# One attention-and-experts kernel on one core: scores moved ahead of the transposes, products of ones in the first groups, and smaller last batches

## The chip, the core and the metric

The kernel runs on one core of one Trainium2 chip. The metric is device time in microseconds. Three runs of the kernel before gave 682.09 us in the median (680.95 to 684.87). All data are float32 in memory.

## What is computed

A blockwise attention over 64-token chunks, then a mixture of eight experts in which each token goes to its best expert only. Cut to what matters:

```python
# attention: batch 8, heads 8, sequence 576, head width 64; chunks of 64 tokens
scores = scale * q_c @ k_c.T                 # 64 x 64 per chunk and head
attn   = exp(scores - max(scores))
attn   = attn / (sum(attn) + 1e-9)
x      = (attn @ v_c) -> [4608 tokens, 512]  # heads side by side

# experts: D = 512, F = 1024, E = 8
logits = x @ w_gate
e      = argmax(logits);  p = softmax(logits)[e]
y      = p * (relu(x @ w1[e]) @ w2[e])
```

## The kernel before, in words

**Tiles and groups.** The 4608 tokens are 36 tiles of 128 rows. Attention works on groups of two tiles, so there are 18 groups. The main loop (L899) runs one turn for each group g, and one turn touches three groups: the scores and softmax of g, the transposes and values of g-1 (called `ga`), and the routing input of g-2 (called `gl`). The order of the instructions on each engine is the order of this code: a manual schedule holds it for TensorE (PE), VectorE (DVE), ScalarE (ACT) and GpSimd (POOL). Each engine works through its own list in order and waits where an input or a buffer is not ready. Transfers of q, k, v and the first expert's weights go out on SP's list, three groups ahead.

**One turn before the change.** PE: transposes of the attention of g-1 (`attn_t`, L265, into the banks T and Q), the routing sums of g-3 (`sel_`, L864), the scores of g (`scores`, L222, into the pair of banks S), the transposes of x of g-2 (`x_t`, L297, again into T and Q), if a batch is due the matmuls of its token places (L369 to L374, into bank K), the products with v of g-1 (`attn_v`, L274, pair X), and the gate logits of g-2 (`logits`, L309). DVE: the row sums of g-1 (`su`, L249), the row maxima of g (`mx`, L235), the subtraction that writes `ex` (L238) and frees the scores' banks, the reciprocal `ri` (L257) and the scaling that writes x of g-1 (`x_out`, L286). ACT: copies out of T and Q (L266 `at`, L299 `xT`), a cast of half a weight chunk (`cast`, L81), the exponential of g (L244), and the copy `lp` of the gate logits (L873), which `sel_` reads one turn later.

**Routing.** When the last group of a batch has passed `sel_`, `route` (L314) is started as a generator. It works out the expert of each token, a place in an expert-sorted buffer `xd`, and the gate, in some 12 small DVE steps, and ends with one indirect DMA per tile on POOL (L406, here called a scatter) that writes the rows of x to `xd`. `BATCHES` gives the tiles of each batch. `advance("c")`, `advance("t")`, `advance("a")` and `pauses()` release steps of the generator that belong to PE or ACT or wait; `small_op(n)` releases up to n of the DVE steps.

**The end of attention.** The first slot of 256 rows (slot 0) is cut into 32 half steps; `filler(n)` lets PE do n of them between the steps of the last routing. After the last route `tables()` finds the rows and the experts of all later slots; POOL then gathers the rows of slot 1 (L508) and loads the weights of slot 2 (L493). From then on slots of 256 rows (some with 64 or 128 extra rows) follow one another to the end: two matrix products in three float32r passes each (L551, L558, L627 to L629), an output row scaled by its gate (L633) and scattered to the output (L634).

Of the kernel before, what the change touches and what calls it, by code (L numbers as in the profile page):

```python
# [8 lines left out]
F32 = mybir.dt.float32  # L9
# [9 lines left out]
P = 128  # L19
NT = 4608  # L20
# [5 lines left out]
NG = NTILE // G  # L26
RB = 4
XB = 5
BATCHES = [4, 8, 8, 4, 4, 4, 4]
NBAT = len(BATCHES)  # L30
NMAX = max(BATCHES)
EARLY = 3
# [13 lines left out]
def attn_moe_kernel(ctx: ExitStack, tc: tile.TileContext, q, k, v, wg, w, out):  # L46
# [86 lines left out]
    pw = bank("X", [P, P])  # L133
    for _ in range(WARM):
        nc.tensor.matmul(pw, ones, ones, start=True, stop=True)
    iota_i = xg[0][0][:, 0:BLK].bitcast(I32)
    nc.gpsimd.iota(iota_i, pattern=[[1, BLK]], base=0, channel_multiplier=0)
    pid_i = xg[0][1][:, 0:NTILE].bitcast(I32)
    nc.gpsimd.iota(pid_i, pattern=[[P, NTILE]], base=0, channel_multiplier=1)
    wg_sb = kv.tile([P, 4, 32], F32, name="wg_sb")  # L140
# [10 lines left out]
        nc.gpsimd.memset(rows_b[:, b:b + 1], float(BATCHES[b] * P))  # L151


    iota_f = const.tile([P, BLK], F32, name="iota_f")
    nc.vector.tensor_copy(iota_f, iota_i)
    pid = kv.tile([P, NTILE], F32, name="pid")
    nc.vector.tensor_copy(pid, pid_i)
# [52 lines left out]
    def quads(i, hp):  # L210
        for c in range(2):
            for m in range(2):
                o = hp * 128 + c * 64
                yield (slice(c * 64, (c + 1) * 64), m, slice((i * 4 + hp) * 64, (i * 4 + hp + 1) * 64),
                       slice(m * 64, (m + 1) * 64), slice(o, o + 64), (m * 64, c * 64))

    def scores(g):
        ps = pair["S"]
        for i in range(G):
            for hp in range(4):  # L220
                for po, m, fo, pi, fi, at_ in quads(i, hp):
                    nc.tensor.matmul(ps[po, m, fo], qt[g][pi, i, fi], kb[g % NK][pi, i, fi],  # L222
                                     start=True, stop=True, tile_position=at_)
        return ps
# [35 lines left out]
    def attn_t(ex):  # L260
        at = sp.tile([P, G, 4, 128], F32, name="at", bufs=1)
        for i in range(G):
            pt = bank("TQ", [P, 4, 128])
            for hp in range(4):
                nc.tensor.transpose(pt[:, hp, :], ex[:, i * 4 + hp, :, :].rearrange("p m k -> p (m k)"), ident)  # L265
            nc.scalar.copy(at[:, i, :, :], pt)  # L266
        return at
# [46 lines left out]
    def route(b, pl):  # L314


        t0, n = first[b], BATCHES[b]
        S3 = [P, n, E]

        xts = [(i, xb[(t0 + i) // RB % XB]) for i in range(0, n, RB)]  # L320
        vec = nc.vector

        def small(name, dt=F32, k=E):
            return sm.tile([P, NMAX, k], dt, name=name, bufs=2)[:, 0:n, :]

        def flat(x):
            return x.rearrange("p t o -> p (t o)")

        ft = sm.tile([P, NMAX, 2], F32, name="ft", bufs=2)[:, 0:n, :]
        nc.gpsimd.tensor_copy(ft[:, :, 1:2], pid[:, t0:t0 + n].unsqueeze(2))  # L330
        yield "c"
        lg = small("lg")
        nc.scalar.copy(lg, pl[:, 0:n, :])
        yield None
        yield "v"
        lm = small("lm", k=1)
        vec.tensor_reduce(flat(lm), lg, AX.X, ALU.max)
        yield "v"
        vec.tensor_tensor(lg, lg, lm.broadcast_to(S3), ALU.subtract)
        yield "v"  # L340
        io3 = iota_m8.unsqueeze(1).broadcast_to(S3)
        eq = small("eq")
        vec.scalar_tensor_tensor(eq, lg, 0.0, io3, ALU.is_equal, ALU.mult)
        yield "v"
        am = small("am", k=1)
        vec.tensor_reduce(flat(am), eq, AX.X, ALU.min)
        yield "v"
        o5 = oh_b[:, b, 0:n + 1, :]
        o4 = o5[:, 0:n, :]
        vec.tensor_tensor(o4, io3, am.broadcast_to(S3), ALU.is_equal)  # L350
        yield "v"
        lo = sm.tile([P, E, NMAX], BF16, name="lo", bufs=2)[:, :, 0:n]
        S8 = [P, E, n]
        vec.tensor_tensor(lo, am.rearrange("p t o -> p o t").broadcast_to(S8),
                          iota_m8.unsqueeze(2).broadcast_to(S8), ALU.is_lt)
        yield "v"
        pfx = sm.tile([P, E], BF16, name="pfx", bufs=2)
        with nc.allow_low_precision("whole numbers"):
            vec.tensor_reduce(pfx, lo, AX.X, ALU.add)
        yield "a"  # L360
        eg = small("eg")
        nc.scalar.activation(eg, lg, AF.Exp)
        yield "t"
        r_live[0] = True
        o = b % 2 * (NMAX + 1) * E
        pr = pR[:, o:o + n * E].rearrange("p (a b) -> p a b", b=E)
        pn = pR[:, o:o + (n + 1) * E].rearrange("p (a b) -> p a b", b=E)

        nc.tensor.matmul(pn, tri, o5, start=True, stop=False)  # L369
        for j in range(n):  # L370
            nc.tensor.matmul(pn[:, j + 1:n + 1, :], ones, o4[:, j:j + 1, :].broadcast_to([P, n - j, E]),
                             start=False, stop=False)
        nc.tensor.matmul(pr, ones, pfx.unsqueeze(1).broadcast_to([P, n, E]), start=False, stop=False)
        nc.tensor.matmul(pn, ones[0:1, :],  # L374
                         rowbase[0:1, b:b + 1].unsqueeze(2).broadcast_to([1, n + 1, E]),
                         start=False, stop=True)
        yield "a"
        nc.scalar.activation(cb[:, b, :], pn[:, n, :], AF.Copy, bias=-float(t0 * P))
        nc.scalar.activation(ce[:, :, b], pn[:, n, :], AF.Copy, bias=-float(t0 * P))
        if b == EARLY - 1:  # L380
            g = early()
            active.append([g, next(g), True])
        if b == NBAT - 1:
            g = tables()
            active.append([g, next(g), True])
        yield "v"
        gs = small("gs", k=1)
        vec.tensor_reduce(flat(gs), eg, AX.X, ALU.add)
        yield "v"
        vec.tensor_scalar(gs, gs, 1e-9, None, ALU.add)  # L390
        yield "v"
        vec.reciprocal(ft[:, :, 0:1], gs)
        yield "v"

        dst = small("dst")
        vec.tensor_tensor(dst, pr, o4, ALU.mult)
        r_live[0] = False
        yield "v"
        di = small("di", I32, 1)
        with nc.allow_low_precision("whole numbers"):  # L400
            vec.tensor_reduce(flat(di), dst, AX.X, ALU.add)
        stored.update(range(t0, t0 + n))
        for i, x in xts:
            nc.gpsimd.tensor_copy(x[:, :, D:D + 2], ft[:, i:i + RB, :])
        for i in range(n):
            nc.gpsimd.indirect_dma_start(  # L406
                out=xds[b % 2 * NMAX + i],
                out_offset=bass.IndirectOffsetOnAxis(ap=di[:, i, :], axis=0),
                in_=xts[i // RB][1][:, i % RB, :], in_offset=None, bounds_check=NT - 1, oob_is_err=False)

    active = []
    r_live = [False]
# [463 lines left out]
    def pauses():  # L876
        for x in list(active):
            if x[1] is None:
                x[1] = next(x[0], "end")
                if x[1] == "end":  # L880
                    active.remove(x)
# [6 lines left out]
    def cast(g):  # L888

        j = g - 2  # L890
        if 0 <= j < 16:
            split_half(j // 2, j % 2, j // 4 % 2)
        j = g + 1
        if 0 < j < 16:
            load_q(j)
# [3 lines left out]
    for g in range(NG):  # L899
        ga, gl = g - 1, g - 2  # L900
        pace[0] = 1000
        if ga >= 0:
            at = attn_t(st_e[ga])
        if gl >= 1:
            sel_(gl - 1)
            advance("c")
        ps = scores(g)
        if gl >= 0:
            st_x[gl] = x_t(gl, xb[gl * G // RB % XB])
        cast(g)  # L910
        if ga >= 0:
            su = soft_c(st_e.pop(ga))
        pauses()
        small_op(5)
        st_e[g] = soft_a(ps)
        soft_b(st_e[g])
        advance("t")
        advance("a")
        small_op(5)
        if ga >= 0:  # L920
            px = attn_v(ga, at)
        logits(gl)
        if ga >= 0:
            ri = soft_d(su)
            x_out(ga, px, ri, xb[ga * G // RB % XB])
        small_op(2)
        advance("a")
        side_op(4)
        if g + 3 < NG:
            load_qk(g + 3)  # L930
        if 3 <= g + 2 < NG:
            load_v(g + 2)

    g = NG - 1
    at = attn_t(st_e[g])
    sel_(g - 2)
    advance("c")
    st_x[g - 1] = x_t(g - 1, xb[(g - 1) * G // RB % XB])
    su = soft_c(st_e.pop(g))
    pauses()  # L940
    small_op(5)
    px = attn_v(g, at)
# [4 lines left out]
    advance("a")  # L947
    make_xt(0, banks="SS")
    sel_(g - 1)
    filler(1)  # L950
    advance("t")
    advance("a")
    st_x[g] = x_t(g, xb[g * G // RB % XB])
    small_op(5)
    filler(2)
    logits(g)
    filler(2)
    sel_(g)
    advance("c")
    pauses()  # L960
    small_op(7)
    advance("a")
    filler(3)
    advance("t")
    advance("a")
    small_op(5)
# [156 lines left out]
```

## Time and profile before

| what | value |
|---|---|
| median of 3 runs | 682.09 us |
| the profiled execution's own time | 682.78 us |
| its span, first to last instruction | 680.9 us |
| PE busy | 604.7 us, 89% of the span |
| DVE busy | 422.2 us, 62% |
| ACT busy | 285.6 us, 42% |
| POOL busy | 262.7 us, 39% |
| first `mx` of attention / last `mx` | 9.0 us / 157.3 us |
| scaling of the last group's x ends | 170.4 us |
| first matmul of slot 1 (L558) | 209.15 us |
| mean granted PE clock | 0.928 |

A timeline row gives the start, the length, the engine, the line, what is written from what, and in brackets how long the engine stood idle just before and what ended that. "issue" and "remote" name no engine of this program as the releaser. A window row gives for one stretch the busy time of each engine, the granted PE clock, the busy share of the DMA engines and their rate. In the records one float32 matmul of the program can show as two, so a `x64` there is the `x32` of the program.

### The profile page before, as it was taken

The numbers are of one execution on the slowest core, as the hardware profiler recorded it, in microseconds if no ns is written. First come the engines' busy times: TensorE is split into PE (matmuls) and PEld (weight loads), VectorE is DVE, ScalarE is ACT, GpSimd is POOL, SyncE is SP. The second block draws the span as 40 slices with busy tenths as digits, with TensorE's granted clock in tenths as the row PEclk, the third lists the DMA queues.
The fourth block names the chain that finished last, engine by engine and source line by source line (L and its number), as shares of the span: only waits on it lengthen the run. The fifth ranks groups of instructions, "written<-read, shape, count | busy, mean of one in ns | idle before, by whom it ended". The sixth has DMA issues, their size and how long they took to land. (4 is left out here: it accounts for less than half of the span.)

```text
span 680.9 us, 14512 instructions
## 1 busy us (share of the span) xinstructions
PE 604.7 (89%) x5757; PEld 529.4 (78%) x5757; DVE 422.2 (62%) x819; ACT 285.6 (42%) x523; POOL 262.7 (39%) x268
## 2 busy tenths in 40 slices
PE   5777878678897979999979999999999999999990
PEld 5566657466787868998859888998899898999980
DVE  5786738484454656776636646667555676667660
ACT  2554426253212334544425434445434444555540
POOL 2123332535261442653315415355313464256331
PEclk7898859697797989999999999999999999999996
DMA  8988857633155532224503612156631126221100
GB/s 311 354 297 275 277 204 252 227 98 116 65 172 210 184 121 96 76 65 161 168 6 128 201 65 59 31 176 204 225 97 34 55 84 230 83 66 34 33 3 31
DMA packets 31872, 94.91 MB, mean 139 GB/s; under 512 B 11456, under 2 KB 11456, under 8 KB 28160
## 3 DMA queue, kind: packets, MB, share of 16 engines
q0 software_dynamic: 20848, 60.74, 26.6%
q1 hardware_dynamic: 10896, 32.53, 13.9%
q8 instruction: 73, 1.20, 0.7%
q14 instruction: 55, 0.45, 0.2%
HBM read 122.65 MB, written 19.82 MB: 209 GB/s over the span
## 5 line engine op out<-in xcount | busy, mean ns | idle before, releaser
L75 DVE TENSOR_TENSOR wlo<-raw,whi 128x1024 fp32r<-128x1024 f32 x134 | 163.7, 1222 | 39.5 <-ACT whi L74 33.1
L493 POOL DMA_INDIRECT raw<-in_w,widx x71 | 72.9, 1026 | 214.4 <-DVE wlo L75 166.9
L74 ACT CAST whi<-raw 128x1024 fp32r<-128x1024 f32 x134 | 140.2, 1046 | 0.1
L571 ACT ACTIVATE hh<-psS 128x256 fp32r<-128x256 f32 x106 | 40.7, 384 | 169.3 <-PE psS L551 89.3
L551 PE MATMUL psS<-xhi,whi 128*128 128x256 f32 x328 | 93.6, 285 | 0.9 <-DVE xlo L534 0.7
L551 PE MATMUL psS<-xhi,wlo 128*128 128x256 f32 x328 | 93.3, 285 | 0.0
L551 PE MATMUL psS<-xlo,whi 128*128 128x256 f32 x328 | 93.3, 284 | 0.0
L576 DVE SCALAR_TENSOR_TENSOR hl<-psS,hh 128x256 fp32r<-128x256 f32 x106 | 44.7, 422 | 70.1 <-ACT hh L571 40.0
L508 POOL DMA_INDIRECT xg<-xd,idx x58 | 77.1, 1329 | 20.2 <-issue 15.8
L551 PEld LDWEIGHTS psS<-xhi,whi 128*128 128x128 f32 x328 | 63.3, 193 | 4.8 <-issue 1.1
L634 POOL DMA_INDIRECT out_y<-y,oid x40 | 49.5, 1237 | 44.1 <-DVE y L633 38.3
L551 PEld LDWEIGHTS psS<-xlo,whi 128*128 128x128 f32 x328 | 63.2, 193 | 2.5
L551 PEld LDWEIGHTS psS<-xhi,wlo 128*128 128x128 f32 x328 | 63.2, 193 | 0.0
L82 POOL TENSOR_TENSOR wlo<-raw,whi 128x512 fp32r<-128x512 f32 x16 | 20.3, 1271 | 92.8 <-ACT whi L81 64.1
L627 PE MATMUL psL<-whi,hh 128*128 128x512 f32 x136 | 55.5, 408 | 0.1
L627 PE MATMUL psR<-whi,hh 128*128 128x512 f32 x136 | 54.3, 399 | 0.0
L628 PE MATMUL psL<-wlo,hh 128*128 128x512 f32 x136 | 54.3, 399 | 0.0
L628 PE MATMUL psR<-wlo,hh 128*128 128x512 f32 x136 | 54.2, 398 | 0.0
L629 PE MATMUL psL<-whi,hl 128*128 128x512 f32 x136 | 53.7, 395 | 0.0
L629 PE MATMUL psR<-whi,hl 128*128 128x512 f32 x136 | 53.7, 395 | 0.0
L235 DVE TENSOR_REDUCE mx<-psS 128x16 f32<-128x1024 f32 x18 | 22.0, 1222 | 42.3 <-PE psS L222 20.2
L222 PE MATMUL psS<-kb,qt 64*64 64x64 f32 x1152 | 32.6, 253 | 10.6 <-issue 8.4
(224 smaller groups left out, 1234.2 us busy)
## 6 DMA issues: line engine op xcount, KB each, us to landing
vb<-in_v SPq DMA_DIRECT2D x18, 512.0 KB, 6.0
kb<-in_k SPq DMA_DIRECT2D x17, 512.0 KB, 5.3
qt<-in_q SPq DMA_DIRECT2D x17, 512.0 KB, 6.0
raw<-in_w SPq DMA_DIRECT2D x16, 256.0 KB, 5.4
raw<-in_w,widx POOLq DMA_INDIRECT x71
xg<-xd,idx POOLq DMA_INDIRECT x58
out_y<-y,oid POOLq DMA_INDIRECT x40
kb<-in_k SPq DMA_DIRECT2D x2, 256.0 KB, 4.4
```

The costliest lines, as they stand in the source:

```text
L74: nc.scalar.copy(hi, src)
L75: nc.vector.tensor_tensor(lo, src, hi.bitcast(F32), ALU.subtract)
L222: nc.tensor.matmul(ps[po, m, fo], qt[g][pi, i, fi], kb[g % NK][pi, i, fi], start=True, stop=True, tile_position=at_)
L493: nc.gpsimd.indirect_dma_start(out=raw[c][:, :], out_offset=None, in_=w, in_offset=bass.IndirectOffsetOnAxis(ap=widx[:, u, c:c + 1], axis= ...
L508: nc.gpsimd.indirect_dma_start(out=t[:, :], out_offset=None, in_=xd[0:rows, :], in_offset=bass.IndirectOffsetOnAxis(ap=place(u, h), axis=0 ...
L551: nc.tensor.matmul(ph, a, b[:, kc, 0:BLK], start=kc + i == 0, stop=kc + i == 5)
L571: nc.scalar.activation(hh, ph, AF.Relu)
L576: nc.vector.scalar_tensor_tensor(hl, ph, 0.0, hh.bitcast(F32), ALU.max, ALU.subtract)
L627: nc.tensor.matmul(py, hh, wh, start=f == 0, stop=False)
L628: nc.tensor.matmul(py, hh, wl, start=False, stop=False)
L629: nc.tensor.matmul(py, hl, wh, start=False, stop=f == 7)
L634: nc.gpsimd.indirect_dma_start(out=outs[m], out_offset=bass.IndirectOffsetOnAxis(ap=oid[u % 3][0:n, m:m + 1], axis=0), in_=y, in_offset=No ...
```

## The change

1. In each turn `scores(g)` stands first. `sel_` of g-3 follows, and only then `attn_t` of g-1, with the row sums of g-1 right behind it. The weight cast stands behind the exponential of g instead of ahead of it, and the first five small DVE steps of a turn, together with `pauses()`, stand behind the subtraction.
2. A new helper `keep(n)` issues n matmuls of ones with ones (128 x 512, bfloat16) into bank K. It runs behind the scores of group 0 with n = 12 and of group 1 with n = 6.
3. The last batch of four tiles becomes two batches of two, with the slices in `route` adapted. `iota_f` shrinks from 256 to 128 columns.
4. Behind the last group the fillers are shared out anew: one half step each between the steps of the last two batches, and the transposes of the last x (`x_t`) come ahead of the first filler.

```diff
-BATCHES = [4, 8, 8, 4, 4, 4, 4]
+BATCHES = [4, 8, 8, 4, 4, 4, 2, 2]
...
+    def keep(n):
+
+        for _ in range(n):
+            nc.tensor.matmul(pR.rearrange("p (a b) -> p a b", b=P), ones,
+                             ones.unsqueeze(1).broadcast_to([P, 4, P]), start=True, stop=True)
...
-        if ga >= 0:
-            at = attn_t(st_e[ga])
+        ps = scores(g)
+        keep((12, 6, 0)[min(g, 2)])
         if gl >= 1:
             sel_(gl - 1)
             advance("c")
-        ps = scores(g)
+        if ga >= 0:
+            at = attn_t(st_e[ga])
+            su = soft_c(st_e.pop(ga))
         if gl >= 0:
             st_x[gl] = x_t(gl, xb[gl * G // RB % XB])
-        cast(g)
-        if ga >= 0:
-            su = soft_c(st_e.pop(ga))
-        pauses()
-        small_op(5)
         st_e[g] = soft_a(ps)
         soft_b(st_e[g])
+        cast(g)
         advance("t")
         advance("a")
+        pauses()
         small_op(5)
...
     make_xt(0, banks="SS")
     sel_(g - 1)
+    advance("t")
+    advance("c")
+    st_x[g] = x_t(g, xb[g * G // RB % XB])
+    advance("a")
+    pauses()
+    small_op(5)
     filler(1)
+    logits(g)
+    small_op(7)
+    advance("a")
+    filler(1)
+    sel_(g)
+    advance("c")
     advance("t")
     advance("a")
-    st_x[g] = x_t(g, xb[g * G // RB % XB])
     small_op(5)
-    filler(2)
-    logits(g)
-    filler(2)
-    sel_(g)
-    advance("c")
     pauses()
+    filler(1)
     small_op(7)
     advance("a")
-    filler(3)
+    filler(1)
     advance("t")
     advance("a")
     small_op(5)
```

The order on PE over one whole turn in the middle of attention, before (psS holds the scores, `ex` the exponentials, xb and vb are x and v):

```order
L265 MATMUL psT<-ident,ex 128x128 x4
L265 MATMUL psQ<-ident,ex 128x128 x4
L864 MATMUL psL<-sel_g,lp 128x8 x2
L222 MATMUL psS<-kb_124,qt 64x64 x32
L297 MATMUL psT<-ident,xb_121 128x128 x4
L297 MATMUL psQ<-ident,xb_121 128x128 x4
L274 MATMUL psX<-vb_126,at 64x64 x32
L309 MATMUL psL<-xT_1056,wg_sb 32x256 x4
```

The same turn on PE in the changed kernel, whose lines stand some six further down:

```order
L228 MATMUL psS<-kb_124,qt 64x64 x32
L870 MATMUL psL<-sel_g,lp 128x8 x2
L271 MATMUL psT<-ident,ex 128x128 x4
L271 MATMUL psQ<-ident,ex 128x128 x4
L303 MATMUL psT<-ident,xb_121 128x128 x4
L303 MATMUL psQ<-ident,xb_121 128x128 x4
L280 MATMUL psX<-vb_126,at 64x64 x32
L315 MATMUL psL<-xT_1079,wg_sb 32x256 x4
```

The scores went from the middle of the turn to its head, the routing sums with them, and the two users of the banks T and Q (L271 and L303) now stand back to back.

ACT over the same turn, before (`at` and `xT` are the copies out of T and Q, `whi` the weight cast, `lp` what the routing sums read):

```order
L266 COPY at<-psT 128x512
L266 COPY at<-psQ 128x512
L299 COPY xT_1056<-psT 128x4x128
L299 COPY xT_1056<-psQ 128x4x128
L81 CAST whi_2_70<-raw_67 128x512
L251 ACTIVATE su<-su 128x16
L244 ACTIVATE ex<-ex 128x1024
L873 COPY lp<-psL 128x256
```

and in the changed kernel:

```order
L272 COPY at<-psT 128x512
L272 COPY at<-psQ 128x512
L257 ACTIVATE su<-su 128x16
L305 COPY xT_1079<-psT 128x4x128
L305 COPY xT_1079<-psQ 128x4x128
L250 ACTIVATE ex<-ex 128x1024
L81 CAST whi_2_70<-raw_67 128x512
L879 COPY lp<-psL 128x256
```

The weight cast moved from ahead of the exponential to between it and `lp`; so `lp`, which the routing sums ahead of the next transposes read, is now one instruction later behind the exponential.

PE behind the last group, before: the routing sums of the last group (L864) and what follows (psS<-xhi and psX<-whi are half steps of slot 0; the token places of the last batch come behind three more such rows):

```order
L864 MATMUL psL<-sel_g,lp 128x8 x2
L551 MATMUL psS<-xhi,whi_2_70 128x256
L551 MATMUL psS<-xlo,whi_2_70 128x256
L551 MATMUL psS<-xhi,wlo_2_78 128x256
L551 MATMUL psS<-xhi,whi_3_71 128x256
L551 MATMUL psS<-xlo,whi_3_71 128x256
L551 MATMUL psS<-xhi,wlo_3_79 128x256
L627 MATMUL psX<-whi_4_72,hh 128x512
L628 MATMUL psX<-wlo_4_80,hh 128x512
L629 MATMUL psX<-whi_4_72,hl 128x512
```

and in the changed kernel (L375 to L380 into psK are token places, here of the last batch but one):

```order
L870 MATMUL psL<-sel_g,lp 128x8 x2
L375 LDWEIGHTS tri
L375 MATMUL psK<-oh_b,tri 128x24
L377 LDWEIGHTS ones
L377 MATMUL psK<-oh_b,ones 128x16
L377 LDWEIGHTS ones
L377 MATMUL psK<-oh_b,ones 128x8
L379 LDWEIGHTS ones
L379 MATMUL psK<-pfx,ones 128x16
L380 LDWEIGHTS ones
L380 MATMUL psK<-rowbase,ones 128x24
```

Behind the last routing sums the places of a batch of two tiles now follow at once, and those of the very last batch after two more half steps. In all, the last batch's places have four half steps of slot 0 ahead of them on PE, where they had eight.

More of the change, by code (lines that the diff above doesn't have):

```diff
@@ L135, in attn_moe_kernel @@
         nc.tensor.matmul(pw, ones, ones, start=True, stop=True)
-    iota_i = xg[0][0][:, 0:BLK].bitcast(I32)
-    nc.gpsimd.iota(iota_i, pattern=[[1, BLK]], base=0, channel_multiplier=0)
+    iota_i = xg[0][0][:, 0:P].bitcast(I32)
+    nc.gpsimd.iota(iota_i, pattern=[[1, P]], base=0, channel_multiplier=0)
     pid_i = xg[0][1][:, 0:NTILE].bitcast(I32)
@@ L151, in attn_moe_kernel @@
         nc.gpsimd.memset(rows_b[:, b:b + 1], float(BATCHES[b] * P))
-    iota_f = const.tile([P, BLK], F32, name="iota_f")
+    iota_f = const.tile([P, P], F32, name="iota_f")
     nc.vector.tensor_copy(iota_f, iota_i)
@@ L318, in route @@
         S3 = [P, n, E]
-        xts = [(i, xb[(t0 + i) // RB % XB]) for i in range(0, n, RB)]
+        xts = [(i, min(RB, n), xb[(t0 + i) // RB % XB], (t0 + i) % RB) for i in range(0, n, RB)]
         vec = nc.vector
@@ L402, in route @@
         stored.update(range(t0, t0 + n))
-        for i, x in xts:
-            nc.gpsimd.tensor_copy(x[:, :, D:D + 2], ft[:, i:i + RB, :])
+        for i, m, x, r in xts:
+            nc.gpsimd.tensor_copy(x[:, r:r + m, D:D + 2], ft[:, i:i + m, :])
         for i in range(n):
@@ L408, in route @@
                 out_offset=bass.IndirectOffsetOnAxis(ap=di[:, i, :], axis=0),
-                in_=xts[i // RB][1][:, i % RB, :], in_offset=None, bounds_check=NT - 1, oob_is_err=False)
+                in_=xb[(t0 + i) // RB % XB][:, (t0 + i) % RB, :], in_offset=None, bounds_check=NT - 1, oob_is_err=False)
     active = []
@@ L934, in attn_moe_kernel @@
     g = NG - 1
-    at = attn_t(st_e[g])
     sel_(g - 2)
     advance("c")
+    at = attn_t(st_e[g])
+    su = soft_c(st_e.pop(g))
     st_x[g - 1] = x_t(g - 1, xb[(g - 1) * G // RB % XB])
-    su = soft_c(st_e.pop(g))
     pauses()
```

## The prediction

> **What bounds the kernel now.** I read the 40 slices first, then windows cut at the starts of the maxima `mx`, one per group.
>
> ```profile
> PE   5777878678897979999979999999999999999990
> PEclk7898859697797989999999999999999999999996
> ```
>
> From the 13th slice on (204 us) PE is busy nine tenths or more nearly throughout. From there to the end the slots pass on PE, and the change touches nothing in them; they move as a block. Whatever is to be won lies ahead of the first slot's matmuls at 209.15 us. There PE is at 5 to 8 tenths.
>
> ```profile
> 17.00:24.00 7.00, 4.50 (x105) 3.88 (x96) 4.79 (x7) 2.23 (x3) 0.00 (x0) 0.76 1.03 409
> 56.00:62.20 6.20, 4.93 (x150) 4.18 (x150) 5.01 (x6) 4.09 (x8) 1.27 (x1) 0.90 0.88 245
> 62.20:69.00 6.80, 5.79 (x162) 4.99 (x163) 6.07 (x12) 4.21 (x9) 1.41 (x2) 1.00 0.89 286
> 75.70:92.70 17.00, 11.95 (x193) 9.24 (x196) 5.97 (x12) 4.22 (x10) 9.37 (x11) 0.70 0.71 247
> 114.70:131.30 16.60, 11.41 (x186) 7.81 (x190) 7.75 (x20) 4.32 (x11) 9.62 (x12) 0.83 0.60 226
> ```
>
> The columns are the window, its length, then busy time of PE, PE's weight loads, DVE, ACT, POOL, the granted clock, the DMA share and GB/s. An undisturbed group takes 6.2 us, in which PE works 4.93 and DVE 5.01: neither is full, so a chain through both sets the pace. A group with routing steps takes 6.8 with DVE at 6.07. And two groups take 17: those in which eight tiles are scattered. The undisturbed group in order of time:
>
> ```profile
> 57.25 1.22 DVE L238 TENSOR_TENSOR ex<-psS,mx 128x1024 f32<-128x1024 f32 x1
> 58.51 1.06 ACT L244 ACTIVATE ex<-ex 128x1024 f32<-128x1024 f32 x1 [0.70 <-DVE ex L238]
> 59.47 0.35 ACT L873 COPY lp<-psL 128x256 f32<-128x256 f32 x1
> 59.62 0.66 PE L265 MATMUL psT<-ident,ex 128*128 128x128 f32 x4 [1.27 <-ACT ex L244]
> 60.37 0.58 ACT L266 COPY at<-psT 128x512 f32<-128x512 f32 x1 [0.54 <-PE psT L265]
> 60.55 0.51 PE L864 MATMUL psL<-sel_g,lp 128*128 128x8 f32 x4
> 60.99 1.16 PE L222 MATMUL psS<-kb,qt 64*64 64x64 f32 x64
> 62.08 0.66 PE L297 MATMUL psT<-ident,xb 128*128 128x128 f32 x4
> 62.22 1.22 DVE L235 TENSOR_REDUCE mx<-psS 128x16 f32<-128x1024 f32 x1 [1.07 <-PE psS L222]
> 63.10 1.16 PE L274 MATMUL psX<-vb,at 64*64 64x64 f32 x64
> 64.20 0.64 PE L309 MATMUL psL<-xT,wg_sb 128*32 128x256 f32 x8
> ```
>
> Subtraction, exponential, transposes, routing sums, scores, maxima, subtraction: 57.25 to 63.5, one group. PE waits 1.27 us for the exponential, DVE 1.07 for the scores. But these scores need nothing of that exponential; only their place behind its transposes makes them wait.
>
> **Term A, the start.**
>
> ```profile
> 8.25 0.69 PE L222 MATMUL psS<-kb,qt 64*64 64x64 f32 x32 [2.11 <-DMA qt<-in_q]
> 12.61 1.22 DVE L249 TENSOR_REDUCE su<-ex 128x16 f32<-128x1024 f32 x1 [1.12 <-ACT ex L244]
> 12.63 1.11 PE L265 MATMUL psT<-ident,ex 128*128 128x128 f32 x4 [3.69 <-ACT ex L244]
> 14.53 1.96 PE L222 MATMUL psS<-kb,qt 64*64 64x64 f32 x64
> 16.56 1.22 DVE L235 TENSOR_REDUCE mx<-psS 128x16 f32<-128x1024 f32 x1 [2.73 <-PE psS L222]
> 202.87 0.39 PE L628 MATMUL psX<-wlo,hh 128*128 128x512 f32 x1
> 203.10 0.39 PE L629 MATMUL psX<-whi,hl 128*128 128x512 f32 x1
> ```
>
> The 12 products start at 8.94 us. Matmuls 512 wide start 0.23 apart at full clock (202.87 and 203.10, far off but the nearest of that width), so 12 take 2.8, and about 5.2 at half. The scores of group 1 follow at 11.7 and take 1.16 (the 60.99 row) instead of 1.96. DVE has its row sums until 13.83, so the maxima start there instead of 16.56: **2.7 us**. At half clock they would start at 8.94 + 5.2 + 1.96 = 16.1: 0.5. The six later products delay the first transposes to about 14, and the cover is that DVE is in maxima and subtraction until 16.3; without that cover they cost 1.4. Bounds 0.5 to 2.7 less 1.4, so -0.9 to 2.7; I take 2.7, because the records show full clock at 8.25 (0.69 us for 32).
>
> The Trainium skill, "TensorE: Matmul & The Clock Gate", Part 1, knows a full and a half clock only, the half one after some 3.4 us idle. PE idles 3.69 us here and its transposes then take 1.11 instead of 0.66, so the trace agrees; by that rule the products hold the clock and the sum keeps its 2.7, and if products of ones did not count as work it would get the 0.5.
>
> **Term B, the ordinary groups.** Scores at the head of the turn take the loop above apart. Three loops are left. DVE: 5.0 of work plus routing steps. PE: pitch between starts 0.93 (transposes) + 0.44 + 1.09 + 1.02 + 1.10 + 0.65 = 5.2; to that comes a new wait, since `x_t` now follows the other transposes directly and needs the banks that `at` copies empty: first bank free at 0.75 + 0.58 = 1.33 behind the first transposes, PE there at 0.93: 0.4. So 5.6 to 5.8. And a chain over two groups: subtraction, exponential, then the new wait of the routing sums for `lp`, which now has the weight cast ahead of it (about 1.0 us behind the exponential), sums 0.44, transposes and copies 1.8, the x transposes, values 1.1, `x_out` 1.2, row sums 1.15, maxima 1.26, subtraction 1.22: 10.8 to 11.5, or 5.4 to 5.8 a group. Queued behind the waiting sums are both transposes and so `at`; the early scores give DVE work meanwhile. So 5.8 against 6.2, with routing steps 6.3 against 6.8; ten such intervals at 0.4 to 0.7: **5 us**. All idle time of DVE in them (say 1.1 each) would be 11; if the `lp` wait and the bank wait are not covered (1.0 + 0.4 against the 1.27 saved) it is -1. I take 5, near the rows of DVE.
>
> **Term C, the scatters.**
>
> ```profile
> 81.21 1.02 POOL L406 DMA_INDIRECT xd<-xb,di  x1 [0.86 <-DVE ri L257]
> 82.52 0.36 PE L222 MATMUL psS<-kb,qt 64*64 64x64 f32 x5 [0.39 <-issue]
> 90.21 0.97 POOL L406 DMA_INDIRECT xd<-xb,di  x1 [0.31 <-issue]
> 92.59 1.76 PE L274 MATMUL psX<-vb,at 64*64 64x64 f32 x51 [0.93 <-issue]
> 92.69 1.22 DVE L235 TENSOR_REDUCE mx<-psS 128x16 f32<-128x1024 f32 x1 [9.55 <-remote]
> 98.87 1.99 PE L222 MATMUL psS<-kb,qt 64*64 64x64 f32 x64
> 100.93 1.22 DVE L235 TENSOR_REDUCE mx<-psS 128x16 f32<-128x1024 f32 x1 [3.05 <-PE psS L222]
> ```
>
> While POOL issues eight scatters, PE gets about five matmuls per 0.7 us, and what waits for it (here the maxima, 9.55 us) starts only after the last: a shadow from 82 to 92.7. It falls on scores just begun. The scatter's time follows from the routing steps behind a subtraction; that subtraction frees the scores' banks. In the new order PE can run the next scores (1.2 us) between the subtraction and the scatter some 2 us later, so maxima and subtraction fall inside the shadow. After it PE has values, logits and the next scores to do: at half clock 1.99 + 0.85 (an estimate, 0.64 at full clock) + 1.99 = 4.8 us to the next maxima, where now it is 100.93 - 92.69 = 8.2. That is 3.4 per long scatter; if copies and x transposes are left over as well (1.1 + 1.9) it is 0.4. The two of four tiles leave less. I take 3 for each of two long ones and 1 for each of two short ones: **8 us**, bounds 0 (the shadow catches the scores as before) to 12.
>
> **Term D, the end of routing.**
>
> ```profile
> 169.15 1.29 DVE L286 TENSOR_TENSOR xb<-psX,ri 128x512 f32<-128x512 f32 x2 [2.89 <-PE psX L274]
> 202.84 0.99 POOL L493 DMA_INDIRECT raw<-in_w,widx  x1 [0.30 <-issue]
> 204.98 0.58 ACT L533 CAST xhi<-psT 128x512 fp32r<-128x512 f32 x1 [2.99 <-PE psX L629]
> 206.34 1.40 DVE L633 TENSOR_SCALAR y<-psX,gate 128x512 f32<-128x512 f32 x2
> 207.99 0.66 PE L540 MATMUL psT<-ident,xg 64*128 64x64 f32 x4 [4.50 <-DVE y L633]
> 209.15 1.44 PE L558 MATMUL psS<-xhi,whi 128*128 128x320 f32 x4 [0.51 <-ACT xhi L542]
> ```
>
> From the last x (170.44) to the slot's first matmul: 38.7 us. PE ends slot 0 at 203.49 and stands 4.5: the cast of 204.98 comes a microsecond after POOL's last weight load, then `y`, the transposes, another cast. The new order puts four half steps instead of eight ahead of the last token places, and the last scatter is two tiles, not four; I work out some 6 us less to the end of POOL's list. The casts then cease to be late and the gap falls from 5.7 to 2.8 (two `y` in 1.4, transposes 0.66, cast and latencies 0.7). PE's own work stays, with less waiting: 1.6. Together **4.5**; between 0 (PE's half steps set the end, as their total is unchanged) and 7 (the half clock at 209, 2.4 us, goes too).
>
> The batch of two adds one routing chain (12 small DVE steps) in the tail, beside half steps on PE; its cover gone, some 3 us. The tables' 64 columns instead of 56 are hidden beside PE. SP's loads keep their places in its list and only start earlier.
>
> **Sum.** 2.7 + 5 + 8 + 4.5 = 20.2. Profiled: 682.78 - 20.2 = 662.6; that execution is 0.7 above the median, so 682.1 - 20.2 = **661.9 us**.
>
> **The rivals.**
>
> *The shadows keep their price.* PE stands with the scores instead of past them, or the transposes left over cost as much: C is 0, 2.7 + 5 + 4.5 = 12.2, 669.9 us. For: the shadow ends where POOL ends, whatever PE holds. Against: the 2 us ahead of it.
>
> *The end moves least.* Attention gets shorter but slot 0's half steps fill the time (D 0), and the new waits eat B and C: only A's lower end remains, 681.5 us, within the measurement. For: DVE is at 89% where routing runs. Against: the rows of 1.27 and 1.07.
>
> *Slower: PE stands without a releaser once per half turn.*
>
> ```profile
> 18.79 0.46 PE L274 MATMUL psX<-vb,at 64*64 64x64 f32 x15 [1.56 <-issue]
> 26.96 0.69 PE L274 MATMUL psX<-vb,at 64*64 64x64 f32 x32 [1.61 <-issue]
> ```
>
> These stops come where the DMA share is 1.03 (the 17 to 24 row), none at 0.88. Faster groups ask for the same bytes in less time. At 1.5 us each, 14 more stops use up all 20.2; one in the scores and one in the values of nine groups ahead of the first long scatter's end, 18 in all, costs 27: 688.7 us. Against: at 5.8 us a group the rate rises by a tenth only. The Trainium skill, "Runtime: NRT & Kernel Launch", Instruction fetch mechanics, calls the refill of instructions mostly hidden; if these stops are refills, the two rows differ from it, and by its rule this rival would cost nothing.
>
> *More.* All bounds at their better ends, C 12, B 7, D 7: 28.7, 653.4 us.
>
> **How the numbers follow.** Forecast 0.58, shadows 0.18, more 0.09, end moves least 0.10, slower 0.05. The predicted time is 661.9; the range 652 to 677 takes in the first three with the uncertainty of C and B and leaves out 0.15 to 0.2. Half a per cent (3.4 us) is about what a measurement of this kernel can tell from no change: faster 0.85, same 0.10, slower 0.05.
>
> **What would show it.** A: the second `mx` near 13.9 and its scores at 1.16. B: `mx` no longer waiting for PE in ordinary groups, intervals of 5.8. C: `mx` and subtraction inside a scatter, the next `mx` about 5 us behind its end. D: POOL's weight loads ended before slot 0's last matmul, a gap near 3. I am wrong if the intervals stay at 6.2, if `mx` still waits 9 us for "remote", or if stops of 1.5 us multiply.

## Result and the profile after

| | before | changed |
|---|---|---|
| median of 4 runs each, one chip | 682.3 us (680.95 to 684.87) | 663.79 us (662.37 to 667.36) |
| ratio, 95% interval | | 0.9732 [0.9684, 0.9781] |
| the profiled execution, its span | 682.78, 680.9 | 663.28, 661.5 |
| again, with the last experiments (chip 8; 11 and 6 runs) | 678.79 us | 664.16 us, 0.9788 [0.9758, 0.9818] |

Faster by 18.5 us, and by 14.6 on chip 8. Of the eleven runs of the kernel before that stand beside the first four experiments (chip 4), one took 968.97 us at a granted clock of 0.553, the others 678.4 to 682.8, and the ratios leave it out. The forecast was 661.9 (652 to 677), so the number held; most of its parts did not. The windows below are cut at the same events in both kernels: the second and the tenth maxima, the end of the last x, the first slot's first matmul, that slot's first product of the second GEMM, the end. Columns: window, length, busy time of PE, weight loads, DVE, ACT, POOL, granted clock, DMA share, GB/s. Before:

```profile
16.56:75.74 59.18, 45.27 (x1232) 38.27 (x1225) 45.61 (x68) 31.64 (x65) 13.42 (x14) 0.93 0.89 309
75.74:170.44 94.70, 75.10 (x1460) 59.39 (x1460) 58.51 (x115) 40.29 (x92) 38.73 (x45) 0.75 0.54 186
170.44:209.15 38.71, 31.56 (x199) 27.89 (x199) 18.53 (x79) 8.14 (x22) 16.91 (x20) 0.85 0.43 152
209.15:216.84 7.69, 7.69 (x37) 7.69 (x37) 2.77 (x14) 1.00 (x4) 0.54 (x1) 0.67 0.60 224
216.84:680.90 464.06, 435.35 (x2658) 387.23 (x2656) 288.62 (x529) 200.92 (x335) 188.32 (x158) 0.98 0.31 100
```

The same windows of the changed kernel:

```profile
15.55:72.78 57.23, 48.85 (x1252) 38.70 (x1251) 44.66 (x67) 32.79 (x68) 13.36 (x14) 0.94 0.90 324
72.78:158.86 86.08, 65.12 (x1457) 49.26 (x1456) 55.98 (x116) 40.24 (x92) 38.82 (x46) 0.87 0.62 206
158.86:198.87 40.01, 32.50 (x205) 27.43 (x203) 20.08 (x90) 8.71 (x28) 16.94 (x21) 0.88 0.48 174
198.87:205.58 6.71, 6.71 (x36) 6.71 (x37) 2.77 (x14) 1.00 (x4) 0.77 (x1) 0.78 0.24 95
205.58:661.50 455.92, 431.40 (x2658) 385.20 (x2656) 289.39 (x529) 200.90 (x335) 195.19 (x158) 0.99 0.31 101
```

Subtracting the lengths gives the ledger of the 19.4 us between the spans:

| stretch | forecast | measured |
|---|---|---|
| to the second maxima (A) | 2.7 | 16.56 - 15.55 = 1.0 |
| second to tenth maxima (B; one short scatter, a part of C, falls into it) | 5, spread over all | 2.0 |
| turns with long scatters, to the last x (C) | 8 | 8.6 |
| end of routing, to the slots' second GEMM (D) | 4.5 | -1.3 + 1.0 = -0.3 |
| the slots | 0 ("they move as a block") | **8.1** |

The largest surprise is the last line: 42% of the gain lies in the part whose instructions the change does not touch.

**Where the slots' 8.1 us are.** The timeline of TensorE at the ends of slots 1 and 5, before. A bracket gives the idle time ahead of the group and its releaser:

```profile
240.93 0.63 PE L531 MATMUL psT<-ident,xg 128*128 128x128 f32 x4 [1.31 <-issue]
241.39 0.49 PE L531 MATMUL psQ<-ident,xg 128*128 128x128 f32 x3
244.03 0.27 PE L531 MATMUL psQ<-ident,xg 128*128 128x128 f32 x1 [2.15 <-issue]
...
350.03 0.63 PE L531 MATMUL psT<-ident,xg 128*128 128x128 f32 x4 [1.74 <-issue]
350.49 0.38 PE L531 MATMUL psQ<-ident,xg 128*128 128x128 f32 x2
353.13 0.44 PE L531 MATMUL psQ<-ident,xg 128*128 128x128 f32 x2 [2.26 <-issue]
...
354.83 0.63 PE L629 MATMUL psR<-whi,hl 128*128 128x512 f32 x1
```

and the same places in the changed kernel:

```profile
229.68 0.63 PE L537 MATMUL psT<-ident,xg 128*128 128x128 f32 x4 [1.32 <-issue]
230.15 0.60 PE L537 MATMUL psQ<-ident,xg 128*128 128x128 f32 x4
...
334.87 0.63 PE L537 MATMUL psT<-ident,xg 128*128 128x128 f32 x4 [1.49 <-issue]
335.33 0.60 PE L537 MATMUL psQ<-ident,xg 128*128 128x128 f32 x4
...
336.24 0.39 PE L635 MATMUL psL<-whi,hl 128*128 128x512 f32 x1
```

Slots 1, 5 and 7 take a form with extra rows, and TensorE leaves it by a jump. Both kernels stop 1.3 to 1.7 us at the jump's target. Before, a second stop of 2.15 and 2.26 us follows seven and six matmuls later, waiting for no engine that the trace names, and the matmuls behind it take 0.63 us instead of 0.39: half clock (granted 0.50 from 245.0 to 248.4 and from 354.3 to 357.7). Lining up equal matmuls of both kernels, the distance between them grows by 3.6 us across the first place and by 4.3 across the second. The changed kernel has no second stop. Since the change adds 21 executed matmuls ahead of the slots, the obvious theory is that the code merely lies elsewhere. That could be tried without touching anything that runs.

### The profile page after: what moved, and what is told of

Its sections match the earlier page's. It is cut to its first block, busy times and chain, and to the rows that moved or that the text cites. A ratio compares the mean times of both kernels' runs of the same rounds, so it can differ in the third digit from the quotient of the medians.

```text
span 661.5 us, 14579 instructions
## 1 busy us (share of the span) xinstructions
PE 596.1 (90%) x5778; PEld 514.9 (78%) x5778; DVE 421.1 (64%) x831; ACT 286.0 (43%) x527; POOL 269.8 (41%) x272
## 5 line engine op out<-in xcount | busy, mean ns | idle before, releaser
L514 POOL DMA_INDIRECT xg<-xd,idx x58 | 80.7, 1391 | 19.8 <-issue 12.5
L640 POOL DMA_INDIRECT out_y<-y,oid x40 | 52.5, 1312 | 46.7 <-DVE y L639 41.1
L280 PE MATMUL psX<-vb,at 64*64 64x64 f32 x1152 | 30.9, 236 | 14.6 <-issue 14.3
L280 PEld LDWEIGHTS psX<-vb,at 64*64 64x64 f32 x1152 | 24.8, 145 | 20.0 <-issue 19.4
```

The costliest lines, as they stand in the source:

```text
L280: nc.tensor.matmul(px[po, m, fo], at[pi, i, hp, po], vb[g % NB][pi, i, fi], start=True, stop=True, tile_position=at_)
L514: nc.gpsimd.indirect_dma_start(out=t[:, :], out_offset=None, in_=xd[0:rows, :], in_offset=bass.IndirectOffsetOnAxis(ap=place(u, h), axis=0 ...
L640: nc.gpsimd.indirect_dma_start(out=outs[m], out_offset=bass.IndirectOffsetOnAxis(ap=oid[u % 3][0:n, m:m + 1], axis=0), in_=y, in_offset=No ...
```

## Experiments

The table holds every run; the last four columns are from the profiled executions. The kernel before was run beside each on the same chip: the first four rows are from chip 4, the next four from chip 12, the last four from chip 8. The chip of the first result is not on record.

| kernel | median us (before) | ratio, interval | second maxima behind first | last x ends | to the slot's first matmul | its second GEMM to the end |
|---|---|---|---|---|---|---|
| before_dead24 | 671.74 (680.38) | 0.9881 [0.9825, 0.9937] | 7.58 | 166.7 | 38.6 | 455.8 |
| after_dead103 | 672.5 (680.38) | 0.9898 [0.9867, 0.9929] | 5.01 | 161.9 | 40.6 | 462.9 |
| order_only | 668.34 (680.38) | 0.9813 [0.9774, 0.9851] | 5.33 | 165.8 | 39.5 | 456.1 |
| tail_only | 669.77 (680.38) | 0.9846 [0.9828, 0.9863] | 7.58 | 168.5 | 39.4 | 455.9 |
| no_products | 641.9 (651.73) | 0.9890 [0.9828, 0.9952] | 5.37 | 143.1 | 34.0 | 455.2 |
| four_more | 651.1 (651.73) | 0.9995 [0.9969, 1.002] | 4.80 | 151.6 | 34.0 | 455.4 |
| cast_first | 639.73 (651.73) | 0.9846 [0.9790, 0.9903] | 4.74 | 138.0 | 35.0 | 456.0 |
| batch_of_four | 642.93 (651.73) | 0.9894 [0.9835, 0.9952] | 4.74 | 143.4 | 31.7 | 458.2 |
| after_again | 664.16 (678.79) | 0.9788 [0.9758, 0.9818] | 5.49 | 159.7 | 40.0 | 455.9 |
| before_again | 676.8, one run (678.79) | | 7.39 | 167.9 | 36.1 | 463.2 |
| cast_first_four | 669.26 (678.79) | 0.9837 [0.9798, 0.9876] | 4.75 | 167.0 | 36.7 | 456.7 |
| light_slot0 | 660.38 (678.79) | 0.9725 [0.9690, 0.9760] | 4.74 | 165.9 | 34.7 | 455.9 |

### Is it the place of the code?

The dead products stand in the form of slot 1 for 128 extra rows, which this input does not take:

```diff
             pe = bank("K", [n, D])
+            if u == 1 and n == EXT:
+                for _ in range(24):
+                    nc.tensor.matmul(pe[:, 0:P], ones, ones, start=True, stop=True)
```

> The kernel before, with 24 products of ones written into the form of slot 1 that this input does not take. What is executed is the same to the last instruction; the code behind that form lies 48 TensorE instructions further on. Theory (place of the code): the second stop of TensorE behind the jump at the end of slot 1 (2.15 us at 244.03) and of slot 5 (2.26 us at 353.13) comes from where the jump's target lies in the code; both go, with the half clock behind them, 8.7 us, so 673.6 us. Rival (these stops belong to the transfers or to the order of the work ahead): nothing changes, 682.3 us.

> The changed kernel, with 103 products of ones in the form of slot 1 that is not taken, so that the jump's targets come to lie, counted modulo 256 TensorE instructions, about where they lay in the kernel before. Theory (place of the code): the two second stops come back, about 2.2 us each and half clock behind them, 663.8 + 8.7 = 672.5 us. Rival (the change removed the stops by its order of work or transfers): 663.8 us, no second stop.

> The kernel before as it is, once more, for a second profile. Theory (the second stops of TensorE come from where the code lies): the stops of 2.15 and 2.26 us stand behind the same matmuls of slots 1 and 5 again, and the slots from the first slot's second GEMM to the end take 464 us. Rival (chance of one execution): other places or none, 456 us.

The kernel before with dead code alone gained 8.6 us, 8.2 of them in the slots (464.06 to 455.8). TensorE behind the same jump of slot 1, no second stop:

```profile
237.29 0.63 PE L531 MATMUL psT<-ident,xg 128*128 128x128 f32 x4 [1.34 <-issue]
237.76 0.60 PE L531 MATMUL psQ<-ident,xg 128*128 128x128 f32 x4
238.11 0.48 PE L627 MATMUL psL<-whi,hh 128*128 128x512 f32 x1
```

The changed kernel with its targets pushed back lost 8.7 us against its first run, 7.0 of them in the slots (455.9 to 462.9), and the stops are there again, though not behind the same matmuls. The first two rows are ten matmuls behind the targets of slots 1 and 5, the third twenty behind that of slot 5:

```profile
235.30 0.50 PE L635 MATMUL psL<-whi,hl 128*128 128x512 f32 x1 [1.84 <-DVE oid L529]
...
343.01 0.50 PE L635 MATMUL psL<-whi,hl 128*128 128x512 f32 x1 [1.38 <-DVE oid L529]
...
347.31 0.36 PE L557 MATMUL psS<-xhi,whi 128*128 128x256 f32 x1 [1.70 <-issue]
```

The name in the first two brackets is the last event ahead of them, not a cause: these products need nothing of `oid`. A second profile of the unchanged kernel before shows its stops behind the very same matmuls:

```profile
236.31 0.49 PE L531 MATMUL psQ<-ident,xg 128*128 128x128 f32 x3
239.10 0.27 PE L531 MATMUL psQ<-ident,xg 128*128 128x128 f32 x1 [2.30 <-issue]
...
347.46 0.44 PE L531 MATMUL psQ<-ident,xg 128*128 128x128 f32 x2 [1.98 <-issue]
```

So the stops belong to the place of the code and not to an execution, and the slots' 8 us are not owed to what the change orders differently. The Trainium skill, "Runtime: NRT & Kernel Launch", Instruction fetch mechanics, says that instructions come in blocks of 256 and that a taken jump out of the window forces a fetch before execution goes on. The first stops of 1.2 to 1.7 us at every jump agree.

The trace also shows the loads themselves. The DMA view lists an instruction queue, q8, whose 73 transfers in the kernel before come to 1.20 MB, 16 KB each. A row gives the transfers that begin in a window, their MB, and their time as a share of 16 engines over the window, here 0.1 us long, so 71.4% is 1.14 us. The kernel before from 241.5 us, the changed one from 230.2, after_dead103 from 232.5:

```profile
q8 instruction: 1, 0.02, 71.4%
...
q8 instruction: 1, 0.02, 96.6%
...
q8 instruction: 1, 0.02, 89.1%
```

In all three a load begins 0.6 us behind the first matmul at the target of slot 1, also where no second stop follows. In the kernel before it ends at 242.67 and TensorE goes on at 244.03; in after_dead103 it ends at 233.95 and TensorE goes on at 235.30: 1.36 and 1.35 us later. In the changed kernel it ends at 231.79, and matmuls follow one another without a stop all the while. From the first slot on, every stop of more than 0.8 us that needs no other engine, in all 14 profiles, ends 1.3 to 1.7 us behind the end of such a load. (That q8 serves TensorE the view does not say; these times do.) So the second stop is a wait for the load that follows the one of the target, and whether it shows depends on how many matmuls TensorE can do meanwhile: 7 and 6 in the kernel before, 10 in after_dead103, enough in the other two. Dead code (48 instructions in one kernel, 206 in the other) changes that number by shifting the target within its block.

### Which part of the change makes the rest?

With the targets laid as in the changed kernel (dead products again), the loop's new order alone, and the new batches and end alone:

```diff
-            at = attn_t(st_e[ga])
+        ps = scores(g)
...
         st_e[g] = soft_a(ps)
         soft_b(st_e[g])
+        cast(g)
```
```diff
-BATCHES = [4, 8, 8, 4, 4, 4, 4]
+BATCHES = [4, 8, 8, 4, 4, 4, 2, 2]
```

> The kernel before with the new order of the loop over groups alone: no products of ones, old batches, old end; 21 products in the form not taken, so that the jump's targets lie as in the changed kernel. Theory: all of the shorter attention but the start is the order's, and it falls on the turns with a scatter: last x near 160.5 us (170.4 before), the ordinary turns no shorter than before, 38.7 us from there to the first slot matmul as before, second stops gone: 682.3 - 10 - 8.7 = 663.6 us. Rival (the short last batches and the new end carry a part): last x as above or later, and 667 to 672 us.

> The changed kernel with the old order in the loop over groups and no products of ones: new batches and new end alone; jump's targets as in the changed kernel. Theory (the end gains nothing): last x at 170.4, 39 to 40 us to the first slot matmul, second stops gone: 682.3 - 8.7 = 673.6 us, within 1. Rival (the term D of the prediction, 4.5 us, holds when it stands alone): 669.1 us.

Eight of the 12.0 and of the 10.6 us are the slots again (456.1 and 455.9 against 464). The order alone brings some 4 us: the turns of the scatters shrink as in the changed kernel (tenth to twelfth maxima 74.18 to 94.84, 20.7 us, against 25.2 before), but the last two groups take 4 us longer, and the last x ends at 165.8, not at 160.5. So the expectation of 10 us there missed. For the end alone the total, 669.8, stands by the rival's 669.1, yet not by its reason: from the last x to the slot's second GEMM it takes 39.4 + 6.9 = 46.3 us, where the kernel before takes 38.7 + 7.7 = 46.4. What it has more than its eight lies near the first long scatter (23.0 us between the tenth and twelfth maxima) and is within the spread that equal code shows in the attention (below).

### The start, the ordinary turns, the cast, the last batch

```diff
-        keep((12, 6, 0)[min(g, 2)])
```
```diff
-        keep((12, 6, 0)[min(g, 2)])
+        keep((12, 6, 4)[min(g, 2)])
```
```diff
+        cast(g)
         st_e[g] = soft_a(ps)
         soft_b(st_e[g])
-        cast(g)
```
```diff
-BATCHES = [4, 8, 8, 4, 4, 4, 2, 2]
+BATCHES = [4, 8, 8, 4, 4, 4, 4]
```

> The changed kernel without the 12 and 6 products of ones; 18 such products in the form of slot 1 that is not taken, so that the code behind lies where it lay. Theory (the early scores make the gain at the start, not the products: without any, the order alone had the second maxima 5.33 us behind the first): second maxima 5.3 to 6.2 us behind the first, 663.8 us within 1.5. Rival (the products hold the clock and with it the gain): second maxima 7 us or more behind the first, 665.2 to 666.4 us.

> The changed kernel with four more products of ones behind the scores of every group from the third on, 0.23 us each at full clock; jump's targets as in the changed kernel. Theory (in ordinary turns TensorE's own round, 5.7 us and its stops, now sets the pace): each of some ten ordinary turns 0.9 us longer, the turns with a scatter not, 671 to 674 us. Rival (VectorE or the loads set the pace, TensorE has room): the products vanish in its waits for the copies (7 us in all), 664 to 666 us.

> The changed kernel with the weight cast ahead of the subtraction and exponential again, as before the change. Theory (the copy of the logits behind the cast costs TensorE only 2.2 us of waits in all, and that is not what bounds): 663.8 us within 1.5. Rival (this wait, named in term B, is what ate term B): 3 to 5 us less, 659 to 661 us.

> The changed kernel with one last batch of four tiles in place of two of two. Theory (TensorE's half steps fill the end whichever way the batches are cut): the first slot's second GEMM begins 46 to 47.5 us behind the last x, as in every kernel so far, 663.8 us within 1.5. Rival (short last batches shorten the end, as term D had it): 2.6 us or more longer there, 666.4 us or more.

These four ran on chip 12, where the kernel before takes 651.73 us; their totals can be held only against each other and against that. Without products the second maxima come 5.37 us behind the first, with them 4.74 to 4.80 there: the products are worth 0.6 us on that chip, the early scores the rest.

Four more products a group cost 8 to 9 us against their neighbours (651.1; 641.9 and 642.93). The windows from the second to the last maxima, without products and with four more:

```profile
14.05:131.71 117.66, 93.17 (x2521) 75.12 (x2522) 93.47 (x163) 66.89 (x144) 43.65 (x49) 0.96 0.83 297
```
```profile
12.76:140.14 127.38, 108.65 (x2591) 83.39 (x2590) 93.74 (x163) 66.32 (x144) 43.80 (x49) 0.93 0.79 279
```

TensorE has 15.5 us more to do, VectorE the same as before, and 9.7 us come out at the end. Turn by turn this bears out neither theory. Of the sixteen turns between the second and the last maxima eight keep their length within 0.1 us, though each holds some 0.9 us more of matmuls: TensorE's round does not set those. The growth sits in three turns, 4.0, 3.3 and 3.9 us (those that end with the fifth, eighth and twelfth maxima), and in each of them TensorE has a stop of 3.2 to 3.6 us that ends 1.3 to 1.4 us behind an instruction load. Without products the two largest such stops (4.0 and 3.7 us) fall one turn later, into those that end with the ninth and thirteenth. How much of the 9.7 us is owed to the loads and how much to TensorE's work was not separated. The cast ahead of the exponential makes 2.2 to 3.2 us less than those two neighbours, but the intervals overlap: neither theory is told apart. With one batch of four the slot's first matmul comes 31.7 us behind the last x instead of 34.0, and its second GEMM 38.5 instead of 39.4, so there the short batches lengthened the end a little; the slots took 2.3 us longer in that kernel, which was not followed up.

### Once more, the two together, and what sets the end

The third kernel leaves the third product out of slot 0's half steps:

```diff
-            for i, (a, b) in enumerate(((wh, xhi), (wh, xlo), (wl, xhi))):
+            for i, (a, b) in enumerate(((wh, xhi), (wh, xlo), (wl, xhi))[:nt]):
...
-        nc.tensor.matmul(py, hl, wh, start=False, stop=f == 7)
+        if nt == 3:
+            nc.tensor.matmul(py, hl, wh, start=False, stop=f == 7)
```

> The changed kernel as it is, once more. Theory (a good part of the gain is in the turns with a long scatter, which exists only where TensorE is held up while GpSimd issues it): 18 us less than the kernel before on a chip where that one takes about 680 us, 9 to 12 less on one where it takes about 652. Rival (the gain does not depend on it): 18 us less on either.

> The changed kernel with the weight cast ahead of the exponential again and one last batch of four. Theory (the cast ahead of the logits' copy cost the turns some 5 us in all, and the short batches cost the end 2 to 3): 3 to 6 us less than the changed kernel on the same chip. Rival (what the turns gain the end gives back, since TensorE's half steps fill it): within 1.5 us of the changed kernel.

> The changed kernel with the third of the three products left out in all half steps of slot 0 (the weights' remainder in its first GEMM, the activations' remainder in its second), 7.5 us of TensorE's work at full clock; jump's targets as in the changed kernel. Theory (TensorE's half steps set the end of the routing): the first slot's first matmul comes 5 to 7.5 us earlier behind the last x, the total as much less. Rival (the chain of routing steps, token places and weight loads sets it): 0 to 2 us less, and TensorE idle in their place.

The changed kernel repeated: 14.6 us faster than before on that chip, where 18 were expected. Cast ahead and one batch of four together were slower than it in the median (669.26 against 664.16, the intervals just overlapping), the opposite of 3 to 6 us less: the last x came at 167.0 instead of 159.7. What was 2 us better on chip 12 does not carry over, so no version that does the whole work was shown to beat the changed kernel.

Without a third of slot 0's products the end shrinks by 5.4 us:

```profile
165.90:200.56 34.66, 26.34 (x153) 21.19 (x154) 19.85 (x90) 8.38 (x26) 16.95 (x21) 0.85 0.41 148
```

Against the 158.86 to 198.87 row TensorE has 32.50 - 26.34 = 6.2 us less to do, and 40.01 - 34.66 = 5.4 come out, with DVE, ACT and POOL busy as before. So TensorE's half steps set the end of the routing. How they are dealt out is not without effect: with one batch of four (cast_first_four) the slot's second GEMM began 43.8 us behind the last x, in the changed kernel on the same chip 46.7. The total of light_slot0 fell by 3.8 us.

## Why the prediction was right, and where it was not

The number was right by luck, because two errors met: terms A, B and D were some 9 us too large, and the slots, put at nothing, gave 8. Held against equal places of the code the change's own order is worth 680.38 - 672.5 = 7.9 us (after_dead103, 0.9898 [0.9867, 0.9929]), 18.5 - 8.1 = 10.4 by the first two profiles, or 14.6 - 7.3 = 7.3 by the two of chip 8 (slots 463.2 and 455.9), where 20.2 was forecast.

**A, the start** (2.7 of 0.5 to 2.7): right in kind, between its bounds in size. The changed kernel:

```profile
9.25 5.14 PE L220 MATMUL psK<-ones 128*128 128x512 bf16 x12
...
14.32 1.16 PE L228 MATMUL psS<-kb,qt 64*64 64x64 f32 x64
...
15.55 1.23 DVE L241 TENSOR_REDUCE mx<-psS 128x16 f32<-128x1024 f32 x1 [1.35 <-PE psS L228]
```

The twelve products took 5.14 us, the half-clock bound of the prediction, not 2.8; the windows give a granted clock of 0.50 from 8 to 14 us. Then the scores took 1.16, as said. The second maxima follow the first by 6.18 us here, by 5.49 in the repeat (products 4.45 us), by 5.01 in after_dead103 and 4.74 in light_slot0; 7.56 before. In after_dead103 the products took 3.98 us, the first six 0.43 us apart, the last six 0.22, with a clock change on record at 10.46 between them. In light_slot0, and in the four other kernels with them, they took what the prediction said for full clock:

```profile
8.74 2.76 PE L220 MATMUL psK<-ones 128*128 128x512 bf16 x12
```

So the gain is 1.4 to 2.8 us, by the clock that the start happens to get, and in the two profiles where most of the products ran at half clock the second maxima came later than without any (5.33 and 5.37 us in order_only and no_products). "The records show full clock at 8.25" was one execution's luck. Nor did the idle time of 3.69 us that the prediction named bring the clock down: in that profile it is 0.50 from 9.50 on, 0.6 us into that time.

**B, the ordinary turns** (5): failed. The failing step is "5.8 against 6.2". The maxima indeed stopped waiting (20.2 us for the scores before, 5.8 after), but second to tenth maxima took 57.23, 59.03 and 57.97 us in the changed kernel, after_dead103 and after_again, and 59.18, 57.69 and 60.97 in the kernel before, before_dead24 and before_again. The 2.0 us of the ledger lie in the turns with the first, short scatter (fifth to eighth maxima: 23.7 to 21.2 us); the seven turns beside the scatter's own took 6.89 us in the mean before and 7.14 after. One ordinary turn of the changed kernel:

```profile
57.01 1.16 PE L228 MATMUL psS<-kb,qt 64*64 64x64 f32 x64
...
58.57 0.63 PE L271 MATMUL psT<-ident,ex 128*128 128x128 f32 x4
...
59.93 0.66 PE L303 MATMUL psT<-ident,xb 128*128 128x128 f32 x4 [0.29 <-ACT at L272]
...
61.01 1.16 PE L280 MATMUL psX<-vb,at 64*64 64x64 f32 x64
...
62.67 0.92 PE L228 MATMUL psS<-kb,qt 64*64 64x64 f32 x45
...
64.45 0.56 PE L228 MATMUL psS<-kb,qt 64*64 64x64 f32 x19 [0.87 <-issue]
...
65.05 1.23 DVE L241 TENSOR_REDUCE mx<-psS 128x16 f32<-128x1024 f32 x1 [0.40 <-PE psS L228]
```

From scores to scores 57.01 to 62.67, 5.66 us: TensorE's pitch is what the prediction worked out (5.6). But a stop of 0.87 us falls into the next scores and the turn is 6.17; others carry stops of 1.29 (24.25 us) and 1.56 (30.63). Each of them ends 1.3 to 1.5 us behind the end of a 16 KB instruction load, and so do the two stops that the prediction shows (18.79 and 26.96): these are refills, and not hidden ones. The turn from the fourth to the fifth maxima, with the stop at 30.63, went from 7.81 to 9.23 us; in after_again it took 10.09, with a stop of 3.15. The prediction's 5.8 had no place for such stops. In the turn shown TensorE waits only 0.29 us for another engine, so there its round is the bound; for other turns four_more speaks against that, and what sets them stays open. The wait for `lp` was not it: 2.2 us in all.

**C, the scatters** (8): right in mechanism, too small in size. Scatter, maxima and subtraction of the changed kernel:

```profile
78.61 1.01 POOL L412 DMA_INDIRECT xd<-xb,di  x1
...
80.14 1.21 DVE L241 TENSOR_REDUCE mx<-psS 128x16 f32<-128x1024 f32 x1
...
87.61 0.98 POOL L412 DMA_INDIRECT xd<-xb,di  x1 [0.30 <-issue]
...
92.99 1.23 DVE L241 TENSOR_REDUCE mx<-psS 128x16 f32<-128x1024 f32 x1 [0.20 <-PE psS L228]
```

The maxima are inside the scatter, the next 4.4 us behind its end (127.25 - 122.2 = 5.1 at the second), as forecast. Tenth to twelfth maxima 25.2 to 20.2 us, fourteenth to sixteenth 24.8 to 20.8: 5.0 and 3.9, more than 3 each; the rest of the stretch, with short scatters put at 1 each, gave back 0.3. The waits for "remote" went from 18.0 to 2.5 us. The first short scatter, in B's stretch, gave 3.7 (sixth to seventh maxima, 10.98 to 7.26) where 1 was put. The three together gave 12.6 us, and 12.0 and 11.6 in the other two pairs of profiles (before_dead24 and after_dead103, before_again and after_again): the prediction's upper bound for C. The other turns gave much of it back: from the second maxima to the last x the three pairs differ by 10.6, 2.9 and 6.6 us only, where B and C had 13.

**D, the end** (4.5): failed. The gap did fall to 2.6 us (196.24 to 198.87), as said:

```profile
197.94 0.43 PE L546 MATMUL psT<-ident,xg 64*128 64x64 f32 x4 [1.70 <-DVE y L639]
```

But "PE's own work stays, with less waiting" was wrong. TensorE's waits ahead of it, by the view of waits:

```profile
PE psT L557 <- DVE hl L582: 1.6, 1, 1.6
PE psS L537 <- DVE xlo L540: 1.4, 1, 1.4
PE psK L375 <- DVE oh_b L356: 1.2, 1, 1.2
PE psT L537 <- DVE hl L582: 1.1, 1, 1.1
```

The half steps' remainders now wait behind routing steps on VectorE; before, only the 1.4 and 0.7 for `xlo` stood ahead of the gap. What went at the end came back in the middle. The prediction's own lower bound (TensorE's half steps set the end, their total unchanged) was the case: light_slot0 shows it. In the other pairs the time from the last x to the slot's second GEMM went from 46.4 to 46.0 and from 43.8 to 46.7 us, so the new end gained nothing and may cost something.

**The slots** (0): "they move as a block" failed; the change moves code, and the dead-code kernels show the 8 us to be that. The rival with multiplying stops was not seen ahead of the slots: the stops without a releaser there sum to 18.8 us before and 19.2 after, and of those over 0.8 us outside the scatters there are three in each (1.56, 1.61, 1.35 and 1.29, 1.56, 0.87). That rival's time is a slip of addition: 661.9 + 27 is 688.9, not 688.7.

## What to carry to other kernels

Where a program jumps, compare the parts that a change does not touch too: dead code in a form that is not taken moves the code and nothing else, and shows what a gain owes to its place; and look up the rows of the instruction queue where an engine stops without a releaser. A wait that is taken away shortens a turn only down to the next limit, so add work to the engine thought free before counting on it, and read the answer turn by turn, since a total can hide that most turns did not move. Where filler work sets the end, having less of it shortens the end; here dealing it out differently did not.

## What the runs showed that was not expected

**One chip does not hold TensorE up during scatters.** On chip 12 the same scatters of eight tiles leave matmuls at full pace (the kernel without products):

```profile
77.86 1.02 POOL L412 DMA_INDIRECT xd<-xb,di  x1
...
81.92 1.16 PE L228 MATMUL psS<-kb,qt 64*64 64x64 f32 x64 [0.54 <-DVE ex L244]
...
86.86 0.97 POOL L412 DMA_INDIRECT xd<-xb,di  x1 [0.30 <-issue]
```

64 matmuls in 1.16 us inside the scatter, where elsewhere five come per 0.7 us. The kernel before takes 651.73 us there instead of 679 to 682, and three of the four variants gain 8.8 to 12.0 us on it, little more than the place of the code is worth elsewhere (8.6 and 8.7). Neither the changed kernel nor a profile of the one before was taken on that chip, so what the change is worth there stays open, and so does why it differs.

**Equal code, other attention.** The last x of the changed kernel's loop ended at 158.9, 159.7, 161.9 and 165.9 us in four profiles; the kernel before's at 170.4, 167.9 and 166.7. Differences of a few microseconds between single profiles in this part prove nothing.
